# An attention block with inducing points and a gated feed-forward layer on one core: the inducing points on another queue, the weight casts on another engine, the next batch's loads placed later, and the written order redrawn

## The chip, the cores and the metric

The kernel runs on one core of a Trainium2 chip. The core has five engines that run side by side, each with its own list of instructions in order: TensorE (PE in the profile; PEld are its weight loads), VectorE (DVE), ScalarE (ACT), GpSimd (POOL) and SyncE (SP), which here only issues transfers. Transfers (DMA) run on 16 engines of their own. The metric is the device time of one execution in microseconds. The result below is judged against runs of the kernel before.

## The reference

Two stages follow each other. In the first, 32 inducing points attend to all 12416 tokens of a batch, giving a summary `h` of 32 rows, and each token then attends to these 32 rows. In the second, each token's result goes through a gated layer with 1536 hidden columns.

```python
def _attn_ref(x, inducing):            # x: 4 x 12416 x 128, inducing: 32 x 128
    def mab(q, kv):
        s = scale * (q @ kv.transpose(0, 2, 1))
        s = s - s.max(-1, keepdims=True)
        a = np.exp(s)
        a /= a.sum(-1, keepdims=True) + 1e-09
        return a @ kv
    h = mab(I, x)
    return mab(x, h)

def _moe_ref(x, w_gate, w_val, w_out): # 128 x 1536, 128 x 1536, 1536 x 128
    gate = 1.0 / (1.0 + np.exp(-(x @ w_gate)))
    val = x @ w_val
    return gate * val @ w_out
```

## The kernel before

**Tiles.** A batch has 97 blocks of 128 tokens. They are worked off as six quads of 16 blocks (the last has 17), and each quad as four units of 512 tokens; the odd block is a short 25th unit. So there are 4 batches of 24 full units and one short one.

**Stages.** For each quad, stage 1 (names `sa`, `hp`) scores the tokens against the inducing points, takes the exponential, and adds the weighted tokens to `hacc`. When all quads of a batch are done, `hT` is the batch's summary, and three folds (`fo`) multiply it with w_gate and w_val into `hw`, so that the second attention and the gated layer's first products become one product with 32 rows. Stage 2 (`sb`) scores the tokens against `hT`; the scores are transposed (`et`), summed by a tree on GpSimd (`tr`), divided (`rc`, `mu`), transposed back (`bt`), written to DRAM (`wr`) and read back four times (`re`), so that four row groups of TensorE can work at once. Then come the units: six products `G` for the gate and twelve `V` for the value, a tanh `T` on ScalarE for each G, a multiplication `D` on VectorE for each V (one in twelve goes through a copy `C` on ScalarE to GpSimd, `P`), twelve products `W` with w_out, a copy `E` and a store `st`.

**Prologue of batch 0.** Here the loads of x come as 32-bit numbers on SP (`lx`), are cast to 16 bits mostly on GpSimd (`cx`), transposed on TensorE (`xt`) and copied back (`xc`). The three weight matrices are loaded on SP too (`lwg`, `lwv`, `lwo`) and cast to 16 bits on GpSimd (`wg`, `wv`, `wo`), the last with a factor of 0.5. The inducing points (`lind`, 16 KB) are loaded on SP; `ind16`, `indT` and `indTc` turn them into the stationary matrix that every first score needs. The rows of quad 0 need no trip through DRAM: `rp` transposes them on TensorE and `rcp` copies them.

**Later batches.** A quad of x is loaded and cast in one transfer on GpSimd's queue (`ld`, into one of four buffers), and transposed by four transfers on SP (`xd`; five for the last quad). Stage 1 of a batch runs between the units of the batch before.

**Order.** Each operation is registered with an engine, a planned duration, its dependencies and a function that emits it. `ORDER` gives every engine's list by hand; `play` walks these lists with the planned durations, finds each operation's planned start, and the kernel emits all operations sorted by it. Each engine thus executes its list exactly as written, and an operation that waits holds up everything behind it on its engine. The waits on the chip themselves come from the data: who writes a tile, who reads it, and when a buffer is free. A dependency that is listed for `play` alone changes planned times, and no wait on the chip.

In the names, `ld1.2` is quad 2 of batch 1, `G0.4.0` the first gate product of unit 4 of batch 0. Every instruction that goes through the helper class `Eng` has line 626 in the profile.

Of the kernel before, what the change touches and what calls it, by code (L numbers as in the profile page):

```python
# [17 lines left out]
QS = 16  # L18
# [7 lines left out]
        xt0.8 xt0.0 indT xt1.8 sa0.0 xt1.0 ap0 xt2.8 sa0.1 xt2.0 hp0.0 ap1 xt3.0 sa0.2 hp0.1 xt3.8 ap2 xt4.0 hp0.2 sa0.3  # L26
        xt4.8 xt5.0 xt5.13 ap3 sa0.4 xt5.8 s1t0 ap4 s1t13 hp0.3 hp0.4 s1t8 hbase hsu0 hva0 hsu8 hva8 hsu13 hva13 s2t1
        s2t0 fo0.0 fo0.2 fo0.1 rp3 sb0.1 rp1 rp0 G0.0.0 V0.0.2 G0.0.1 V0.0.1 V0.0.8 G0.0.4 G0.0.5 V0.0.9 sa1.0 V0.0.0
        G0.0.2 G0.0.3 rp2 W0.0.2 V0.0.4 V0.0.5 G0.1.1 V0.0.7 G0.1.0 W0.0.8 W0.0.0 V0.1.0 G0.2.0 V0.0.3 V0.0.6 W0.0.4
        G0.1.5 G0.1.2 V0.0.11 V0.0.10 W0.0.9 V0.1.2 V0.1.5 G0.1.3 W0.0.11 sb0.2 W0.0.6 V0.1.3 V0.1.4 G0.2.3 V0.1.6  # L30
        W0.0.10 W0.0.7 G0.2.1 V0.1.10 W0.0.5 G0.1.4 V0.1.1 W0.0.1 V0.2.2 V0.1.7 G0.3.0 W0.0.3 V0.1.11 V0.2.7 V0.2.0
        G0.3.3 W0.1.1 W0.1.3 W0.1.4 G0.2.2 V0.1.8 W0.1.11 G0.2.5 V0.1.9 V0.2.5 W0.1.8 W0.1.9 G0.2.4 V0.2.4 hp1.0 G0.3.2
        V0.2.1 W0.1.7 W0.1.6 V0.3.0 V0.2.3 G0.3.4 W0.1.10 V0.2.9 W0.1.5 W0.1.0 V0.3.4 G0.3.1 V0.2.6 W0.1.2 V0.3.3 V0.3.2
        G0.3.5 V0.2.10 W0.2.4 W0.2.1 V0.2.8 V0.3.5 G0.4.0 W0.2.7 V0.4.0 G0.4.4 W0.2.8 W0.2.6 W0.2.0 G0.4.1 V0.2.11
        W0.2.2 V0.3.1 V0.3.6 G0.4.5 W0.2.10 W0.2.9 W0.2.3 G0.4.2 V0.3.8 W0.2.5 V0.4.2 V0.3.7 W0.2.11 sa1.1 V0.4.3 V0.4.4
        G0.4.3 W0.3.2 V0.4.1 W0.3.7 V0.3.9 G0.5.0 W0.3.5 V0.3.10 G0.5.1 V0.3.11 W0.3.3 W0.3.1 V0.4.6 G0.6.0 V0.4.9
        W0.3.0 W0.3.10 V0.4.5 G0.5.5 W0.3.4 W0.3.8 V0.4.7 G0.5.2 V0.4.8 W0.3.9 W0.3.11 W0.3.6 V0.4.10 V0.5.1 sb0.3
        G0.6.1 W0.4.4 W0.4.0 V0.5.5 G0.5.3 V0.5.0 V0.5.6 W0.4.6 W0.4.5 sa1.2 W0.4.7 V0.4.11 G0.6.3 V0.5.2 W0.4.8 W0.4.2
        G0.7.0 V0.5.3 V0.5.11 W0.4.1 V0.5.4 V0.5.7 G0.5.4 W0.4.10 W0.4.9 W0.4.3 V0.6.3 V0.6.2 G0.7.3 V0.5.10 W0.4.11
        V0.6.0 G0.6.2 V0.5.9 V0.5.8 V0.6.7 G0.6.4 W0.5.0 W0.5.1 W0.5.8 G0.6.5 V0.6.4 V0.6.5 W0.5.7 W0.5.5 G0.7.4 V0.6.1  # L40
        W0.5.6 hp1.1 G0.7.2 V0.6.6 W0.5.2 W0.5.10 G0.7.1 V0.7.0 V0.6.11 W0.5.4 W0.5.9 W0.5.11 W0.5.3 V0.7.4 V0.6.9
        G0.7.5 sa1.3 V0.7.2 W0.6.11 W0.6.3 V0.7.3 G0.8.0 V0.6.8 W0.6.7 V0.6.10 W0.6.2 V0.7.5 V0.8.0 G0.8.1 W0.6.6 W0.6.1
        V0.7.8 G0.8.4 W0.6.8 W0.6.4 V0.7.1 G0.8.5 V0.8.2 W0.6.10 W0.6.0 W0.6.5 W0.6.9 V0.8.1 G0.8.2 V0.7.7 G0.8.3 V0.7.6
        W0.7.1 W0.7.2 W0.7.8 V0.8.4 V0.8.3 W0.7.3 G0.9.0 V0.7.10 W0.7.4 G0.9.1 V0.7.9 V0.7.11 W0.7.10 W0.7.6 V0.8.5
        G0.10.0 V0.8.7 W0.7.0 G0.9.5 V0.8.9 W0.7.7 G0.9.2 V0.8.8 V0.8.6 W0.7.5 W0.7.11 W0.7.9 V0.9.0 G0.9.3 V0.9.1 sb0.4
        V0.8.10 W0.8.0 W0.8.3 V0.9.5 V0.9.2 G0.10.1 W0.8.2 hp1.2 sa1.4 V0.8.11 G0.10.3 V0.9.11 W0.8.5 V0.9.6 G0.11.0
        W0.8.4 W0.8.1 G0.10.2 V0.9.7 V0.9.4 W0.8.11 W0.8.7 W0.8.8 G0.9.4 V0.9.10 W0.8.6 V0.10.2 V0.9.3 W0.8.9 W0.8.10
        V0.9.8 G0.11.3 V0.10.3 G0.10.5 V0.10.0 W0.9.1 W0.9.4 V0.10.5 V0.10.4 W0.9.6 W0.9.5 W0.9.7 V0.9.9 G0.10.4 V0.10.7
        W0.9.0 V0.10.1 G0.11.4 W0.9.8 hp1.3 G0.11.1 V0.10.6 W0.9.11 W0.9.3 V0.11.0 V0.10.11 G0.11.2 W0.9.2 W0.9.10
        W0.9.9 G0.11.5 V0.10.9 V0.11.4 sa1.5 V0.11.2 W0.10.6 W0.10.2 V0.11.3 G0.12.0 V0.10.8 W0.10.5 W0.10.3 V0.10.10  # L50
        W0.10.1 V0.11.5 G0.12.1 V0.11.8 W0.10.0 W0.10.4 V0.12.0 G0.12.4 W0.10.9 W0.10.7 V0.11.1 V0.12.2 G0.12.5 W0.10.8
        W0.10.10 W0.10.11 V0.12.1 V0.11.6 G0.12.2 G0.12.3 V0.11.7 W0.11.1 W0.11.0 W0.11.2 V0.11.10 G0.13.0 V0.12.4
# [1105 lines left out]
```

## Time and profile before

| | |
|---|---|
| median of three runs | 737.59 us (733.43 to 741.64) |
| the profiled execution, its time | 733.21 us |
| the profiled execution, its span | 731.4 us |
| busy in it: TensorE, VectorE, ScalarE, GpSimd | 679.9, 677.7, 681.0, 342.6 us |
| mean granted TensorE clock | 0.984 |

The span is cut into 40 slices of 18.3 us on the profile's page, with the busy share of each engine in tenths. A line of the chain of waits gives start, duration and what was going on; a line of the timeline gives start, time from the first to the end of the last of the merged instructions, engine, operation and tiles (out<-in), and in brackets how long the engine had stood before, and what ended it. In a list of transfers the last number is the microseconds from issue to landing. SPq and POOLq are the issuing instructions of a queue.

### The profile page before, as it was taken

The page shows a single profiled execution, that of the slowest core. Times are in us where ns is not written, and L with a number is a line of the kernel's source. Part 1 is how long each engine was busy: PE and PEld are TensorE (multiplying, and loading weights), DVE is VectorE, ACT ScalarE, POOL GpSimd, SP SyncE. Part 2 cuts the span into 40 slices and gives each one's busy share as a digit, 9 for nine tenths or more (in the row PEclk, how much of TensorE's full clock was granted, in tenths as well). Part 3 has the DMA queues.
Part 4 walks back from the last instruction along what each step waited for, and adds up shares of the span by engine and source line. Part 5 has one row for each costly group of instructions (what it writes and reads, how often), then busy time and mean ns, then how long its engine had stood idle before and what let it go on. Part 6 is the DMA issues. An engine that isn't in the chain of part 4 may idle for free.

```text
span 731.4 us, 20034 instructions
## 1 busy us (share of the span) xinstructions
PE 679.9 (93%) x7928; PEld 381.4 (52%) x7928; DVE 677.7 (93%) x1156; ACT 681.0 (93%) x881; POOL 342.6 (47%) x452
## 2 busy tenths in 40 slices
PE   1749999999999999999999999999999999999997
PEld 0514555555555555555555555555545555555555
DVE  0448999999999999999999999999999999999997
ACT  1449999999999999999999999999999999999994
POOL 6335562562653552653644635526355345436332
PEclk9958999999999999999999999999999999999999
DMA  9594568665264754554545382331232221332111
GB/s 362 149 131 86 104 151 182 119 113 120 74 154 87 152 137 95 118 120 99 117 129 98 78 155 86 92 104 34 83 93 69 78 80 45 95 93 63 35 73 48
DMA packets 113327, 78.63 MB, mean 107 GB/s; under 512 B 80561, under 2 KB 97361, under 8 KB 112593
## 3 DMA queue, kind: packets, MB, share of 16 engines
q1 hardware_dynamic: 110640, 67.81, 37.0%
q0 software_dynamic: 2592, 9.54, 8.1%
q8 instruction: 62, 1.02, 0.6%
q14 instruction: 33, 0.26, 0.1%
HBM read 39.99 MB, written 28.57 MB: 94 GB/s over the span
## 4 chain that ended last, share of the span: by engine, by line
PE 50%; DVE 20%; ACT 15%; DMA 6%; issue 6%; POOL 2%; SPq 1%; ACTq 0%; POOLq 0%; DVEq 0%
PE acc L626 24%; DVE ua L626 19%; PE v L626 17%; ACT tga L626 12%; PE g L626 8%; DMA ind<-in_inducing_dram 2%; DMA xT<-x 2%; ACT os L626 2%; DMA out_dram<-os 1%; ACT vs L626 1%; SPq L626 1%; DMA xT<-in_x_dram 1%; POOL pt L626 1%; POOL ua L626 1%; ACT eT L626 0%
## 5 line engine op out<-in xcount | busy, mean ns | idle before, releaser
L626 DVE SCALAR_TENSOR_TENSOR ua<-tga,v 128x512 f16<-128x512 f16 x1056 | 648.5, 681 | 18.7 <-PE g L626 7.5
L626 ACT ACTIVATE tga<-g 128x1024 f16<-128x1024 f32 x576 | 562.4, 1078 | 5.1 <-PE v L626 1.8
L626 PE MATMUL acc<-wo,ua 128*128 128x128 f16 x4608 | 360.6, 221 | 2.0 <-DVE ua L626 0.3
L626 PEld LDWEIGHTS <-ua 128*128 128x128 f16 x4608 | 261.8, 98 | 172.6 <-issue 162.7
L626 PE MATMUL v<-a2r,hw 32*128 32x512 f16 (+1 forms) x1200 | 329.2, 376 | 12.5 <-DVE ua L626 10.0
L626 POOL TENSOR_TENSOR pt<-tga,vs 128x512 f32<-128x512 f16 x96 | 111.7, 1164 | 294.4 <-ACT vs L626 167.0
L626 PE MATMUL g<-a2r,hw 32*128 32x512 f16 (+1 forms) x1200 | 227.1, 380 | 4.1 <-ACT tga L626 2.0
L626 PEld LDWEIGHTS <-hw 32*128 32x128 f16 x2400 | 89.5, 91 | 116.4 <-issue 49.3
L626 POOL TENSOR_TENSOR ua<-pt,vs 128x512 f16<-128x512 f32 x96 | 121.7, 1268 | 7.5
L626 ACT COPY os<-acc 128x512 f32<-128x512 f32 (+1 forms) x100 | 62.3, 623 | 7.1 <-PE acc L626 6.7
L626 ACT COPY vs<-v 128x512 f32<-128x512 f32 x96 | 60.4, 630 | 0.2 <-PE v L626 0.2
L626 POOL TENSOR_TENSOR a2n<-e2t,rc 128x128 f16<-128x128 f16 x96 | 37.2, 484 | 18.3 <-DVE rc L626 17.5
L626 ACT ACTIVATE eT<-g 128x512 f16<-128x512 f32 (+1 forms) x26 | 15.5, 609 | 22.7 <-PE g L626 22.7
L626 POOL TENSOR_TENSOR tree<-e2t 128x256 f32<-128x256 f16 (+1 forms) x23 | 15.8, 687 | 24.2 <-DMA e2t<-e 24.2
L626 POOL TENSOR_TENSOR tree<-tree 128x64 f32<-128x64 f32 (+4 forms) x69 | 23.7, 344 | 5.4
L626 DVE CAST ind<-ind 32x128 f16<-32x128 f32 x1 | 0.2, 214 | 19.7 <-DMA ind<-in_inducing_dram 19.7
L626 ACT ACTIVATE e<-g 128x512 f16<-128x512 f32 (+1 forms) x23 | 16.2, 703 | 0.0
L626 PE MATMUL g<-xT,indT 128*32 128x512 f16 (+1 forms) x104 | 11.1, 393 | 5.3 <-DMA xT<-x 5.0
L626 POOL DMA_DIRECT2D x<-in_x_dram x18 | 10.6, 590 | 11.5 <-PE g L626 5.8
L626 PE MATMUL v<-ident,x 128*128 128x128 f16 x97 | 9.4, 258 | 6.9 <-POOL x L626 6.9
L626 ACT CAST hw<-g 128x1024 f16<-128x1024 f32 x11 | 11.7, 1076 | 0.8 <-PE g L626 0.7
L626 PEld LDWEIGHTS <-x 128*128 128x128 f16 x114 | 7.9, 113 | 8.6 <-POOL x L626 7.1
(77 smaller groups left out, 155.8 us busy)
## 6 DMA issues: line engine op xcount, KB each, us to landing
out_dram<-os SPq DMA_DIRECT2D x96, 256.0 KB, 2.3
a2r<-dr SPq DMA_DIRECT2D x92, 128.0 KB, 3.0
x<-in_x_dram POOLq DMA_DIRECT2D x15, 512.0 KB, 5.6
xT<-in_x_dram SPq DMA_DIRECT2D x3, 1024.0 KB, 9.0
dr<-a2p SPq DMA_DIRECT2D x19, 128.0 KB, 1.9
x<-in_x_dram POOLq DMA_DIRECT2D x3, 544.0 KB, 5.9
xT<-x SPq DMA_TRANSPOSE x75, 2.8
tga<-in_x_dram SPq DMA_DIRECT2D x1, 1024.0 KB, 5.0
```

The costliest lines, as they stand in the source:

```text
L626: ins = fn(*a, **k)
```

## The change

1. The inducing points are loaded by a transfer on ScalarE's queue, first in its list, instead of the tenth on SP's.
2. The weights are cast by ScalarE (two copies and one activation with scale 0.5) instead of GpSimd. In ScalarE's list `wg` stands behind `xsa0.4`, `wv` and `wo` behind the exponentials of stage 1's last quad and ahead of `xsb0.1`.
3. The loads of batch 1 get other planned conditions: quads 0 and 1 behind the cast of w_out, quads 2 to 5 behind the first tanh of units 0, 3, 6 and 9.
4. Planned durations and landings are changed, `play` keeps the loads of the prologue in the order of their registration, and all lists are redrawn. The starts of the lists, cut to what the text speaks of:

```diff
 "PE"
-xt0.8 xt0.0 indT xt1.8 sa0.0 xt1.0 ap0
+xt0.0 xt0.8 xt1.0 xt1.8 indT sa0.0 xt2.0
...
-ap3 sa0.4 xt5.8 s1t0 ap4 s1t13 hp0.3 hp0.4 s1t8 hbase hsu0 hva0 hsu8 hva8 hsu13 hva13 s2t1 s2t0 fo0.0 fo0.2 fo0.1 rp3 sb0.1 rp1 rp0
-G0.0.0 V0.0.2 G0.0.1 V0.0.1 V0.0.8 G0.0.4 G0.0.5 V0.0.9 sa1.0
+xt5.0 sa0.4 xt5.13 ap3 hp0.2 ap4 s1t8 s1t13 hp0.3 hp0.4 s1t0 hbase hsu0 hva0 hsu8 hva8 hsu13 hva13 sb0.1 fo0.1 s2t1 s2t0 fo0.2 fo0.0 rp0 rp1
+G0.0.2 V0.0.4 G0.0.0 V0.0.1 V0.0.0 G0.0.4 G0.1.2 G0.0.1 V0.0.8 V0.0.9 W0.0.4
...
+G0.1.4 V0.1.8 W0.1.7 V0.3.3 W0.1.4 W0.1.1 sa1.0
 "ACT"
-xc0.8 xsa0.0 xc1.8 xsa0.1
+lind xc0.8 xc1.8 xsa0.0 xsa0.1
...
-xs2t1 xs2t0 fc0.0 fc0.2 rcp3 xsb0.1 rcp1 T0.0.0 T0.0.1 T0.0.4 T0.0.5 xsa1.0
+xsa0.4 wg xs1t8 xs1t13 xs1t0 wv wo xsb0.1 xs2t1 xs2t0 fc0.2 fc0.0 rcp1 T0.0.2 T0.0.0
...
+C0.1.3 xsb0.2 T0.2.4 T0.2.0 rcp3 E0.0 T0.2.3 T0.3.0 T0.2.1 T0.3.1 T0.1.4 C0.3.3 xsa1.0
 "DVE"
-hr0 hc0 es1 er1 es0 en1 er0 en0 fc0.1 rcp0 D0.0.2
+hr0 hc0 fc0.1 es0 er0 es1 en0 er1 en1 rcp0 D0.0.4
 "POOL"
-cx5.0 cx5.8 ld1.0 ld1.1 wg ld1.2 wv wo ld1.3 tr0.1 mu0.1 P0.0.3 P0.1.3 tr0.2 P0.2.3 mu0.2 P0.3.3 P0.4.3 ld1.4
+cx5.8 cx5.0 ld1.0 ld1.1 tr0.1 mu0.1 ld1.2 P0.0.3 P0.1.3 ld1.3 tr0.2 P0.2.3 P0.3.3 mu0.2 P0.4.3 ld1.4
 "SP"
-lx4.0 lx5.8 lx5.0 lx5.13 lwg lind lwo lwv xd1.0.2 xd1.0.0 xd1.0.3 xd1.0.1 et0.1 xd1.1.0 xd1.1.2 xd1.2.3 at1.0
+lx4.0 lx5.0 lx5.8 lx5.13 lwg lwv lwo et0.1 xd1.0.3 xd1.0.1 bt0.1 xd1.0.2 xd1.0.0 xd1.1.0 wr0.1 et0.2 xd1.1.2 xd1.2.3 re0.1.2
```

The code around the lists:

```diff
-                if any(d.start is None for d in o.deps):
+                if any(d.start is None for d in o.deps) or (o.behind and o.behind.start is None):
...
-        return op("SP", 0.6, [], name, lambda o: SP.dma_start(dst, src), tail=max(2.0, landed[0] - landed[1]))
+        loads.append(op("SP", 0.6, [], name, lambda o: SP.dma_start(dst, src), tail=max(2.0, landed[0] - landed[1]), behind=loads[-1]))
+        return loads[-1]
...
+            if b == 0 and p == 0 and u % 3 == 0:
+                paced[2 + u // 3] = a
...
-    ld = load(ind32[:], inducing, 40000, "lind")
+    ld = op("ACT", 0.6, [], "lind", lambda o: ACT.dma_start(ind32[:], inducing), tail=3.0)
...
-        wl[nm] = op("POOL", 1.7, [ld], nm, lambda o, n=n, dst=dst: POOL.tensor_copy(out=dst, in_=WS[n]))
+        wl[nm] = act(F, [ld], nm, lambda o, n=n, dst=dst: ACT.copy(out=dst, in_=WS[n]))
...
-    wl["wo"] = op("POOL", 2.3, [ld], "wo", lambda o: POOL.tensor_scalar(
-        out=wo[:].rearrange("p j c -> p (j c)"), in0=WS[2], scalar1=0.5, scalar2=None, op0=ALU.mult))
+    wl["wo"] = act(F, [ld], "wo", lambda o: ACT.activation(
+        out=wo[:].rearrange("p j c -> p (j c)"), in_=WS[2], func=AF.Copy, scale=0.5))
...
-                    load_quad(b, i, [c for _, _, c in xload[0, NQ - 1][1]] if b == 1 else [])
+                    load_quad(b, i, ([wl["wo"]] if i < 2 else [paced[i]]) if b == 1 else [])
```

The other planned values that change are durations of the prologue's products on TensorE (from 0.08 to between 0.026 and 0.056 us for each block, and the like) and landings of transfers.

More of the change, by code (lines that the diff above doesn't have):

```diff
@@ L25 @@
     "PE": """
[L26 to L40, printed above, removed]
@@ L299 @@
-        C3.22.3 T3.22.5 T3.22.4 T3.23.4 T3.23.2 C3.23.3 E3.21 T3.24.1 T3.23.1 T3.23.5 T3.24.0 E3.22 E3.23 E3.24
+        lind xc0.8 xc1.8 xsa0.0 xsa0.1 xc2.8 xc3.8 xsa0.2 xc4.8 cx5.15 xsa0.3 xc5.8 xsa0.4 wg xs1t8 xs1t13 xs1t0 wv wo
+        xsb0.1 xs2t1 xs2t0 fc0.2 fc0.0 rcp1 T0.0.2 T0.0.0 T0.0.4 T0.1.2 T0.0.1 T0.0.3 C0.0.3 T0.0.5 T0.1.1 T0.1.0 T0.1.5
+        T0.1.3 C0.1.3 xsb0.2 T0.2.4 T0.2.0 rcp3 E0.0 T0.2.3 T0.3.0 T0.2.1 T0.3.1 T0.1.4 C0.3.3 xsa1.0 T0.2.2 C0.2.3
+        T0.2.5 E0.1 T0.3.3 T0.3.4 T0.3.5 T0.3.2 T0.4.0 T0.4.1 T0.4.4 T0.4.5 T0.4.2 E0.2 T0.4.3 T0.5.0 C0.4.3 xsa1.1
@@ L995 @@
     vcount = [0]
-    evac = []
+    evac, paced = [], {}
     def unit(b, u):
```

783 lines of the change are left out of this document (397 added, 386 removed).

## The prediction

> **What bounds the kernel now.** I read the slices of the page first, then busy time in chosen stretches, then the chain that ended last.
>
> ```profile
> span 731.4 us, 20034 instructions
> ...
> ACT  1449999999999999999999999999999999999994
> ```
> ```profile
> core 0: us, PE busy (x) PEld busy (x) DVE busy (x) ACT busy (x) POOL busy (x), PEclk, DMA share, GB/s
> 8.90:21.20 12.30, 0.03 (x1) 0.03 (x1) 0.30 (x2) 0.05 (x1) 5.44 (x6) 1.00 1.03 399
> ...
> 49.12:55.02 5.90, 0.87 (x7) 0.23 (x6) 0.74 (x2) 0.00 (x0) 0.17 (x1) 0.50 1.31 154
> 60.00:700.00 640.00, 622.76 (x7192) 346.51 (x7192) 631.15 (x1071) 636.45 (x818) 310.04 (x406) 1.00 0.44 102
> 700.00:731.40 31.40, 27.29 (x332) 17.37 (x330) 26.16 (x43) 21.19 (x27) 7.30 (x6) 0.97 0.12 45
> ```
>
> From 60 us to 700 us ScalarE is busy 636.45 of 640 us: it is the bound there, and a new order of the same work can win back 3.55 us at most. What is loose lies ahead of 60 us: in 8.90 to 21.20 TensorE, VectorE and ScalarE all stand, and in 49.12 to 55.02 ScalarE does nothing. The chain names both waits:
>
> ```profile
> 8.22 12.66 DMA ind<-in_inducing_dram
> ...
> 20.90 0.23 DVE ind L626
> ...
> 41.77 12.46 DMA xT<-x
> ...
> 54.27 0.67 PE g L626 x3
> ```
>
> First the 16 KB of inducing points; then a transposing transfer of the next batch, for whose scores (sa1.0) TensorE waits with batch 0 queued behind.
>
> **Part 1: the inducing points on ScalarE's queue.** Before, they are the tenth transfer on SP's queue.
>
> ```profile
> 0.74 1.28 ACT L626 ACT_TABLE_LOAD   x1 [0.74 <-PEq L1142]
> ...
> 2.94 2.04 SPq L626 DMA_DIRECT2D ua<-in_x_dram  x4
> ...
> 5.73 0.33 SPq L626 DMA_DIRECT2D tga<-in_moe_w_gate_dram  x1
> ...
> 8.22 0.34 SPq L626 DMA_DIRECT2D ind<-in_inducing_dram  x1
> ...
> 10.74 2.03 POOL L626 CAST x<-xT 128x1024 f16<-128x1024 f32 x2 [0.45 <-DMA xT<-in_x_dram]
> ...
> 13.18 4.91 SPq L626 DMA_DIRECT2D tga<-in_moe_w_val_dram  x1
> ```
> ```profile
> tga<-in_moe_w_gate_dram SPq DMA_DIRECT2D x1, 768.0 KB, 14.9
> ...
> tga<-in_moe_w_val_dram SPq DMA_DIRECT2D x1, 768.0 KB, 12.0
> ...
> ua<-in_x_dram SPq DMA_DIRECT2D x1, 256.0 KB, 14.2
> ```
>
> After, they are ScalarE's first instruction. It can go out at 0.74 us, or at 2.02 behind the table load. It lands at the latest after the 12.66 us that it took before, so by 14.7, and I take that it lands with the first load of x, by 5.8 (the load of w_gate goes out at 5.73, when that one is done), because nothing is queued ahead of it. TensorE's new list asks for it after four transposes of quads 0 and 1; quad 1 is cast when quad 2's cast begins, at about 10.5. So nothing waits for it, and no instruction of ScalarE is late: its first copy needs a transpose.
>
> [...] No row of before has a transfer on ScalarE's queue.
>
> With the points there, quads 0 to 3 are worked off as they land, one per 2.5 us, each cast in 2.03 us. The new end of the prologue is set by the last piece of x: the last of four issues in 2.94 to 4.98 starts near 4.5, plus 14.2 gives 18.7. From there I use rows of the old ending:
>
> ```profile
> 29.51 0.94 DVE L626 CAST x<-ua 128x512 f16<-128x512 f32 x3
> 29.62 0.41 ACT L626 CAST x<-ua 128x256 f16<-128x256 f32 x1
> ...
> 30.70 0.75 POOL L626 DMA_DIRECT2D x<-in_x_dram  x1 [0.99 <-PE g L626]
> ...
> 34.66 0.54 POOL L626 DMA_DIRECT2D x<-in_x_dram  x1 [3.21 <-PE acc L626]
> ...
> 36.89 0.29 DVE L626 TENSOR_TENSOR hT<-acc,rsb 128x128 f16<-128x128 f32 x1
> ...
> 37.73 0.66 ACT L626 ACTIVATE eb<-v 128x384 f16<-128x384 f32 x2 [2.41 <-PE v L626]
> ...
> 38.55 4.12 POOL L626 TENSOR_SCALAR wo<-hw 128x1536 f16<-128x1536 f32 x1
> ...
> 39.06 1.93 ACT L626 CAST hw<-g 128x1024 f16<-128x1024 f32 x2 [0.68 <-PE g L626]
> 39.13 3.09 DVE L626 TENSOR_TENSOR nb<-eb,rb 128x384 f16<-128x384 f16 x1
> ...
> 42.34 0.29 DVE L626 TENSOR_TENSOR nb<-eb,rb 128x128 f16<-128x128 f16 x1
> 42.55 1.22 DVE L626 CAST hw<-g 128x1024 f16<-128x1024 f32 x1
> ...
> 44.22 0.42 DVE L626 COPY a2r<-v 128x512 f16<-128x512 f16 x1 [0.46 <-PE v L626]
> ```
> ```profile
> 45.35 3.77 ACT L626 ACTIVATE tga<-g 128x1024 f16<-128x1024 f32 x4 [0.84 <-PE v L626]
> ```
>
> 18.7 plus VectorE's three casts (0.94) is 19.6. Before, hT was done (36.89 + 0.29 = 37.18) 6.73 us after the last cast (30.45); the same again gives 26.4.
>
> **Part 2: the weights on ScalarE.** One cast: the 1024-wide ones to hw take 0.97 each (1.93 / 2), the 256-wide cast 0.41, so 0.73 ns per element and 1.34 us for 1536; three cost about 4.0 us. All lie ahead of the first tanh, where ScalarE has gaps, so the stretch from 60 us on gets none of it. w_gate lands at 5.73 + 14.9 = 20.6, before ScalarE asks. That cast stands ahead of the last three exponentials of stage 1; it may push hT from 26.4 to 27.8 (upper bound), and nothing if it falls in a gap, which I take. The third weight is now w_out; the last weight landed at 13.18 + 12.0 = 25.2, and I use that. ScalarE's list has the w_out cast ahead of the next exponentials (xsb0.1, xs2t1, xs2t0), so these wait for 25.2 + 1.34 = 26.5 or later. What GpSimd gives up: two casts and the 4.12 us cast of w_out, which ran beside VectorE's nb of 3.09 us, where the piece a third as wide took 0.29; without it I count 3 x 0.29 = 0.87 for nb, bounded by 3.09.
>
> **Part 3: the next batch's loads.** The new conditions (behind the w_out cast, behind a paced tanh) enter only the planned times: emission uses the written list, the buffers' readers and data. So loads 1.0 and 1.1 keep their place right behind the last casts on GpSimd, and go out when hp0.2 and hp0.3 free their buffers (before: 30.70 and 34.66, the second 2.5 us ahead of hT). After, I put them at 23 and 24. They then share the DMA engines with w_out, of which up to 25.2 - 23 = 2.2 us are left; shared by halves these take twice as long: w_out lands at 25.2 at the best, 27.4 at the worst; I take 26.4, as the first load also needs time to start. The cast ends at 27.7, xsb0.1 costs about 0.5, with a gap the exponentials (eb) begin at 28.8 (bounds: 27.1 without either delay, 29.6 with both), and end 0.66 later, 29.5. VectorE then has two sums, two reciprocals and two products: 0.55 before for the wide sum (next fence), 0.6 together for the three small ones (an estimate by their widths), 0.29 + 0.87 for the products, 2.3 in all: 31.8. From the copy of a2r to the first tanh it was 45.35 - 44.22 = 1.13. **First tanh at 32.9** (bounds 31.2 and 33.7) instead of 45.35: 12.45 us earlier.
>
> ```profile
> 38.25 0.55 DVE L626 TENSOR_REDUCE sb<-eb 128x12 f32<-128x384 f16 x1 [1.06 <-ACT eb L626]
> ```
>
> The fold that VectorE copies (1.22) now stands ahead of those sums; it begins about when hT and two products of TensorE are done, near 28, and ends by 29.3, under eb.
>
> Load 1.2 really is later: behind mu0.1 instead of between weight casts; 1.3 to 1.5 stand behind products of units 1, 4 and 7.
>
> **Part 4: the new table.** TensorE's list has sa1.0 after 18 G's instead of 4. Four tanhs took 3.77 us, so 18 take 17.0, and ScalarE's list has six shorter pieces between (three copies, an exponential, a row copy, one output), 0.41 for 256 elements and 0.19 for 256 more, 0.6 each: the wait would come at 32.9 + 20.6 = 53.5. The transposes that it needs are placed behind et0.1 and around bt0.1 on SP:
>
> ```profile
> 36.14 7.17 SPq L626 DMA_TRANSPOSE xT<-x  x4
> ...
> 54.85 0.66 POOL L626 TENSOR_TENSOR tree<-e2t 128x256 f32<-128x256 f16 x1 [11.65 <-DMA e2t<-e]
> ...
> 60.22 1.55 POOL L626 TENSOR_TENSOR a2n<-e2t,rc 128x128 f16<-128x128 f16 x4 [3.18 <-DVE rc L626]
> ```
> ```profile
> x<-in_x_dram POOLq DMA_DIRECT2D x4, 512.0 KB, 9.0
> xT<-x SPq DMA_TRANSPOSE x8, 9.0
> e2t<-e SPq DMA_TRANSPOSE x1, 10.7
> ```
>
> The landings in the second fence are those of 30 to 60 us, with four loads in flight. Worst: et0.1 goes out at 28.3 and lands 10.7 later, at 39; tree, reciprocal and products take what they took from 54.85 to 61.77, 6.9, then bt0.1 and the last two transposes are issued (7.17 / 4 = 1.8 each, 5.4), and the last needs 9.0 to land: 60, which is 6.8 too late, and that wait would be as long as the old one. With two loads in flight rather than four I halve both landings: about 51, in time, by little. I take that nothing is left of the 5.90 us. Late next is then the replicated rows of unit 4 (re0.1), on the same chain. rcp3, a row copy of 0.6 us on ScalarE, moves behind the first tanh: +0.6. For the remaining order I take 0: it can win 3.55, and the list keeps its distances (35 to 40 G's between a quad's second score and its first use, in both tables, from batch 1 on).
>
> **Sum.** The profiled execution took 733.21 us, 1.8 above its span of 731.4. 733.21 - 12.45 - 5.90 + 0.6 = 715.5. The four known executions (733.21, 733.43, 737.59, 741.64) have their middle at 735.5, 2.3 above the profiled one, which the runs of after should share: **718 us** against the median of 737.59.
>
> **Rivals.**
> - A, the wait moves: SP's list is in order and stands at bt0.1 until GpSimd's products are done, and again at transposes of load 1.2. If that chain is as slow as in the rows with four loads, sa1.0 or the first G of unit 4 stops TensorE for up to 6.8 us, more than the 5.90 removed; at the worst the forecast plus 6.8: 725. For it: landings of 9.0 and 10.7. Against: fewer loads in flight.
> - B, the move to ScalarE's queue brings only the issue time: the points land 12.66 us after 2.02, at 14.7, and the 16.3 us of work that followed them before (20.90 to 37.18) put hT at 31.0, 4.6 later than counted: 723. [...] For it: the 12.66 us themselves. Against: those were spent behind megabytes issued earlier on the same queue.
> - C, slower than before: the new table makes ScalarE wait in the long stretch. It runs 96 full units, and decides at (737.6 - 718) / 96 = 0.20 us per unit; for slower by over 1%, 0.28. Before, ScalarE's idle time there was 3.55 us, 3.55 / 92 = 0.04 per unit of the some 92 in it. For it: every list is redrawn, and VectorE has only 8.85 us free in 640. Against: the same work and distances. At 0.3 per unit it gives 747; half of this, 732.
>
> **How the numbers follow.** Forecast 0.60, A 0.20, B 0.08, C 0.12 (0.07 within 1%, 0.05 slower). The runs of before lie 8.2 us apart, so about 1% (730.2 to 745.0) is what can be told from no change. Forecast, A and B are faster by more: 0.88. Low end: first tanh at 31.2 (-1.7), 3.5 won in the long stretch, a run like the profiled one: 710, and 709 for rounding of the parts. High end: A with a run as far up as the highest (8.4): 715.5 + 6.8 + 8.4 = 731, of which I leave off the last 2, where both mishaps must meet: 729. It leaves out C and a remnant of A.
>
> **What would show it.** The points' landing before 10 us and no stretch of 12 us without TensorE; w_out's cast on ScalarE near 27 and nb under 1 us; loads 1.0 and 1.1 on GpSimd near 23, not after the w_out cast; the first tanh at 31 to 34; no gap over 1 us on ScalarE from there to 60; and idle time of about 3.5 us per 640 from then on. Wrong it would be through a gap at sa1.0 or unit 4, or through idle time spread over all units.

## The result, and the profile after

| | before | after |
|---|---|---|
| median, us | 735.51 (733.25 to 741.64, 4 runs) | 714.11 (712.57 to 714.54, 4 runs) |
| the profiled execution, its time and span | 733.21, 731.4 | 714.31, 712.5 |
| its mean granted TensorE clock | 0.984 | 0.988 |

After takes 0.9692 of the time of before (95% interval 0.9627 to 0.9758): 3% less. The forecast was 718 us, the range 709 to 729. In the experiments below the medians go over all executions, the ranges leave out two at 838.33 us (experiment 2) and 814.6 us (experiment 7), and the ratios leave out every execution in a slow state, so that a median and its ratio need not match.

The page of after, its span, ScalarE's busy tenths in 40 slices of 17.8 us, and the granted clock of TensorE in the same slices:

```profile
span 712.5 us, 20005 instructions
...
ACT  3989999999999999999999999999999999999994
...
PEclk9959999999999999999999999999999999999999
```

The first three slices, 1 4 4 before, are 3 9 8. The 5 in the last row is taken up below. Busy times of after in chosen stretches (columns as in the prediction's first such table):

```profile
10.00:20.00 10.00, 9.20 (x118) 6.50 (x116) 4.91 (x10) 5.64 (x11) 7.32 (x9) 1.00 1.02 417
...
25.00:30.00 5.00, 3.31 (x62) 1.79 (x61) 3.05 (x8) 4.63 (x7) 0.00 (x0) 1.00 0.97 189
30.00:35.00 5.00, 2.92 (x47) 0.94 (x47) 2.93 (x6) 4.64 (x6) 1.89 (x5) 0.95 0.49 93
35.00:40.00 5.00, 5.00 (x50) 2.16 (x46) 3.62 (x7) 4.39 (x6) 1.41 (x4) 0.50 0.02 5
40.00:45.00 5.00, 5.00 (x37) 2.39 (x36) 3.63 (x7) 3.95 (x5) 3.04 (x4) 0.50 0.74 110
45.00:50.00 5.00, 4.65 (x47) 2.11 (x43) 3.16 (x6) 4.04 (x7) 2.99 (x4) 0.50 1.04 170
...
31.65:60.00 28.35, 26.00 (x232) 12.27 (x230) 21.05 (x34) 25.69 (x33) 13.84 (x23) 0.70 0.72 118
...
60.00:681.00 621.00, 604.53 (x7033) 338.21 (x7029) 614.66 (x1043) 618.42 (x794) 297.24 (x389) 1.00 0.44 102
```

TensorE now works 9.20 of the 10 us from 10 to 20 in which it stood before. From 60 us on ScalarE is idle for 621 - 618.42 = 2.6 us, as little as before. The timeline of after, with the lines that answer to the quoted ones of before:

```profile
0.74 0.42 ACTq L625 DMA_DIRECT2D ind<-in_inducing_dram  x1
...
10.75 0.39 SPq L625 DMA_DIRECT2D hw<-in_moe_w_out_dram  x1
...
18.87 1.60 DVE L625 CAST x<-ua 128x512 f16<-128x512 f32 x3
...
23.23 1.37 POOL L625 DMA_DIRECT2D x<-in_x_dram  x2 [2.91 <-PE v L625]
...
26.23 0.29 DVE L625 TENSOR_TENSOR hT<-acc,rsb 128x128 f16<-128x128 f32 x1
26.24 1.48 ACT L625 ACTIVATE wo<-hw 128x1536 f16<-128x1536 f32 x1 [0.23 <-DMA hw<-in_moe_w_out_dram]
...
28.10 0.65 ACT L625 ACTIVATE eb<-v 128x384 f16<-128x384 f32 x2
28.23 1.32 SPq L625 DMA_TRANSPOSE e2t<-e  x1
...
30.10 0.56 DVE L625 TENSOR_TENSOR nb<-eb,rb 128x384 f16<-128x384 f16 x1
...
31.65 1.95 ACT L625 ACTIVATE tga<-g 128x1024 f16<-128x1024 f32 x2
31.88 0.67 POOL L625 TENSOR_TENSOR tree<-e2t 128x256 f32<-128x256 f16 x1 [7.28 <-DMA e2t<-e]
```
```profile
55.07 0.64 ACT L625 ACTIVATE eT<-g 128x512 f16<-128x512 f32 x1
```

The first tanh starts at 31.65 instead of 45.35: 13.70 us won. The exponential of sa1.0 (55.07) has no bracket, so ScalarE did not wait for it. And the transfers up to 30 us, the last number being us from issue to landing:

```profile
hw<-in_moe_w_out_dram SPq DMA_DIRECT2D x1, 768.0 KB, 15.5
...
ind<-in_inducing_dram ACTq DMA_DIRECT2D x1, 16.0 KB, 3.5
```

Where the time went, in the two profiled executions: up to the first tanh 13.70 us; from there to the end 731.4 - 45.35 = 686.05 against 712.5 - 31.65 = 680.85, so 5.20 us, which is the 5.90 us wait less the 0.6 us of rcp3, to 0.1 us. Two other things cancel within it. From the first tanh to 60 us ScalarE of after is idle for 28.35 - 25.69 = 2.66 us, nearly all of it while the granted clock is 0.50, where before it was idle for 0.59 us beside the wait; from 60 us to the end it is idle for 11.82 us, before for 13.76. Together 18.9 us. The medians lie 21.4 us apart; the 2.5 us between these two figures come from which execution was profiled, 2.3 us below the median in before and 0.2 us above it in after. TensorE's clock may make such differences (experiment 6), but for these runs it is not shown: the clocks of before's other executions are not known.

### The profile page after: what moved, and what is told of

The parts are those of the page before. It is cut to its first block, busy times and chain, and to the rows that moved or that the text cites. A ratio compares the mean times of both kernels' runs of the same rounds, so it can differ in the third digit from the quotient of the medians.

```text
span 712.5 us, 20005 instructions
## 1 busy us (share of the span) xinstructions
PE 679.3 (95%) x7928; PEld 382.2 (54%) x7928; DVE 677.4 (95%) x1156; ACT 685.2 (96%) x884; POOL 336.5 (47%) x449
## 4 chain that ended last, share of the span: by engine, by line
PE 56%; DVE 27%; ACT 11%; issue 5%; DMA 1%; POOL 0%; ACTq 0%; SPq 0%; DVEq 0%
PE acc L625 27%; DVE ua L625 25%; PE v L625 20%; PE g L625 9%; ACT tga L625 8%; ACT os L625 2%; DMA xT<-in_x_dram 1%; ACT vs L625 1%; DVE ut L625 1%; ACT eT L625 0%; ACT hw L625 0%; ACT tgt L625 0%; ACT e L625 0%; DVE xT L625 0%; DVE hw L625 0%
## 5 line engine op out<-in xcount | busy, mean ns | idle before, releaser
L625 DVE SCALAR_TENSOR_TENSOR ua<-tga,v 128x512 f16<-128x512 f16 x1056 | 648.7, 680 | 13.7 <-PE v L625 3.7
L625 ACT ACTIVATE tga<-g 128x1024 f16<-128x1024 f32 x576 | 562.0, 1078 | 3.5 <-PE v L625 1.0
L625 PE MATMUL acc<-wo,ua 128*128 128x128 f16 x4608 | 362.4, 221 | 1.3
L625 PEld LDWEIGHTS <-ua 128*128 128x128 f16 x4608 | 262.6, 98 | 170.1 <-issue 160.9
L625 PE MATMUL v<-a2r,hw 32*128 32x512 f16 (+1 forms) x1200 | 327.6, 377 | 12.4 <-DVE ua L625 9.6
L625 POOL TENSOR_TENSOR pt<-tga,vs 128x512 f32<-128x512 f16 x96 | 111.7, 1164 | 296.8 <-ACT vs L625 208.6
L625 PE MATMUL g<-a2r,hw 32*128 32x512 f16 (+1 forms) x1200 | 227.0, 381 | 4.7 <-ACT tga L625 3.1
L625 PEld LDWEIGHTS <-hw 32*128 32x128 f16 x2400 | 89.7, 91 | 120.3 <-issue 55.7
L625 POOL TENSOR_TENSOR ua<-pt,vs 128x512 f16<-128x512 f32 x96 | 121.8, 1268 | 7.5
L625 ACT COPY os<-acc 128x512 f32<-128x512 f32 (+1 forms) x100 | 62.3, 623 | 6.8 <-PE acc L625 6.8
L625 ACT COPY vs<-v 128x512 f32<-128x512 f32 x96 | 60.9, 634 | 1.6 <-PE v L625 1.2
L625 POOL TENSOR_TENSOR a2n<-e2t,rc 128x128 f16<-128x128 f16 x96 | 37.2, 485 | 25.2 <-DVE rc L625 22.2
L625 POOL TENSOR_TENSOR tree<-tree 128x64 f32<-128x64 f32 (+4 forms) x69 | 23.8, 344 | 5.4
L625 POOL TENSOR_TENSOR tree<-e2t 128x256 f32<-128x256 f16 (+1 forms) x23 | 15.9, 690 | 20.2 <-DMA e2t<-e 20.2
L625 ACT ACTIVATE eT<-g 128x512 f16<-128x512 f32 (+1 forms) x26 | 15.7, 613 | 1.6 <-PE g L625 1.5
L625 PE MATMUL v<-ident,x 128*128 128x128 f16 x97 | 9.8, 270 | 7.4 <-POOL x L625 7.4
L625 ACT ACTIVATE e<-g 128x512 f16<-128x512 f32 (+1 forms) x23 | 15.8, 687 | 0.0
L625 DVE COPY xT<-v 128x1024 f16<-128x1024 f16 (+1 forms) x7 | 4.5, 651 | 11.7 <-PE v L625 11.6
L625 ACT COPY xT<-v 128x1024 f16<-128x1024 f16 (+1 forms) x6 | 5.8, 959 | 9.4 <-PE v L625 9.4
L625 PEld LDWEIGHTS <-x 128*128 128x128 f16 x114 | 8.4, 119 | 9.0 <-POOL x L625 8.5
L625 POOL DMA_DIRECT2D x<-in_x_dram x18 | 10.7, 596 | 3.0 <-PE v L625 2.9
L625 ACT CAST hw<-g 128x1024 f16<-128x1024 f32 x11 | 11.6, 1059 | 0.1
```

Source lines behind the costliest of these rows:

```text
L625: ins = fn(*a, **k)
```

## The experiments

Each ratio is to runs of before on the same chip. L625 to L639 in the lines is the helper class in each kernel's own numbering. "Half clock" stands for stretches in which the granted clock is 0.50; a mean clock c over a span s is worth about 2 x (1 - c) x s us of it (0.988 over 712.5 us gives 17.1 us for after, whose profile has 0.50 from 34.5 to 51.6).

**1. The points alone (`e1_points`).** Before, and only:

```diff
-    ld = load(ind32[:], inducing, 40000, "lind")
+    ld = op("ACT", 0.6, [], "lind", lambda o: ACT.dma_start(ind32[:], inducing), tail=3.0)
 "ACT"
+lind xc0.8 xsa0.0 ...
 "SP"
-lx5.13 lwg lind lwo lwv
+lx5.13 lwg lwo lwv
```

> The kernel before, with the inducing points alone moved: first in ScalarE's list, on ScalarE's queue. Theory (three waits in a row, each worth its own time): the first tanh comes near 34.5 us instead of 45.35, since the weight casts on GpSimd still run beside nb; the wait at sa1.0 stays, 6 to 9 us, because the next batch's loads and transposes move forward with the prologue. About 723 us. Rival (the points save only issue time): they land near 14.7 us and the time is 726 to 728. Rival (the next batch's loads now collide with the weights, so that the gain is eaten): first tanh near 39, 728 or more.

724.39 us (722.12 to 726.69), ratio 0.9802 (0.9727 to 0.9877). The first tanh came at 36.16, 9.2 us earlier. The total was as expected, but not the way to it. ScalarE's timeline:

```profile
36.16 3.77 ACT L638 ACTIVATE tga<-g 128x1024 f16<-128x1024 f32 x4 [0.84 <-PE v L638]
39.83 0.60 ACT L638 ACTIVATE eT<-g 128x512 f16<-128x512 f32 x1
```

The exponential of sa1.0 follows the first four tanhs without a bracket: the wait is gone, though the score stands where it stood. What was lost instead lay at the old cast of w_val on GpSimd (TensorE stood 3.7 us for it ahead of a fold) and in a longer half clock, from 40 to about 63 us, in which ScalarE had gaps (busy 7.52 of 10 us from 50 to 60). So the points' queue is the larger part of the gain: some 16 us of medians on this chip (740.4 for before; 14.7 by the ratio), of 21.

**2. The weight casts alone (`e2_weights`).** Before, with the three casts as ScalarE's, at `xsa0.4 wg xs1t0` and `xs1t13 wv wo xs2t1` in its list, and taken out of GpSimd's.

> The kernel before, with the three weight casts alone moved from GpSimd to ScalarE. Theory: nb falls from 3.09 us to under 1, the first tanh comes about 2 us earlier (43.2), but sa1.0 still waits for transposes that land near 54, so the time is the same as before within 1 us. Rival (the gain of 2 us goes through to the end): 2 us less than before.

733.96 us (728.05 to 738.61), ratio 0.9966 (0.9919 to 1.0013): no difference that can be told. The first tanh came 0.64 us earlier (44.71) and ScalarE's wait at sa1.0 shrank from 5.9 to 3.3 us, but the half clock lasted until about 71 us. The product nb took 0.54 us, as expected, but ScalarE's casts now stand ahead of the exponentials eb, which began at 39.30 instead of 37.73: most of what nb won was lost again there.

**3. The score later (`e3_late_score`).** Before, with sa1.0 and its exponential 14 gate products later, as in after:

```diff
 "PE"
-G0.0.5 V0.0.9 sa1.0 V0.0.0
+G0.0.5 V0.0.9 V0.0.0
...
+W0.1.4 G0.2.2 sa1.0 V0.1.8
 "ACT"
-T0.0.5 xsa1.0 T0.0.2
+T0.0.5 T0.0.2
...
+T0.3.3 T0.2.2 xsa1.0 T0.2.5
```

(hp1.0, ha1.0 and at1.0 are put later in the same manner.)

> The kernel before, with sa1.0 alone moved from after 4 gate products to after 18 (its exponential, its transpose at1.0 and hp1.0 behind it). Theory: the gap of 5.9 us at 49 us goes; the rows of unit 4, which landed near 75.6, come up to 2 us late next, so the time falls by 4 to 6 us. Rival (the wait only moves): a gap of 4 us or more at the first product of unit 4, and under 2 us gained.

738.28 us (732.03 to 742.94), ratio 0.9972 (0.9924 to 1.0019): the 4 to 6 us did not come. Its timeline shows the wait elsewhere:

```profile
55.93 0.66 POOL L638 TENSOR_TENSOR tree<-e2t 128x256 f32<-128x256 f16 x1 [12.47 <-DMA e2t<-e]
...
58.16 0.25 DVE L638 RECIPROCAL rc<-sm 128x16 f32<-128x16 f32 x1 [4.50 <-POOL sm L638]
...
61.03 1.02 ACT L638 ACTIVATE tga<-g 128x1024 f16<-128x1024 f32 x1 [3.65 <-PE g L638]
```

Read upwards: ScalarE waited 3.65 us for TensorE, because VectorE stood 4.50 us at the reciprocal of quad 1, because GpSimd's tree waited for the transposed scores, which landed 11 us after their issue, four loads being in flight. This is the prediction's rival A, at another operation than it named. The rest went into half clock, up to 78 us (ScalarE is busy 14.58 of the 20 us from 60 to 80 at a mean clock of 0.55, in before 19.68 at 1.00).

**4. The three together, in the old lists (`e4_three`).** The edits of 1, 2 and 3 in one kernel. GpSimd's list then has four loads of batch 1 side by side.

> The kernel before, with these three edits together, but without the redrawn table and with the next batch's four loads where they were on GpSimd (now directly behind each other, as no weight cast is between them). Theory: the three edits carry the gain and the redrawn table nothing: 714 to 717 us, first tanh near 32.5. Rival (the later place of loads 1.2 and 1.3 counts): with four loads in flight the transposes land late, a gap of 3 us or more at sa1.0 or unit 4, 719 or more.

722.34 us (720.49 to 724.77), ratio 0.9766 (0.9707 to 0.9825). The first tanh came at 37.10, not at 32.5, and the list of ScalarE's waits between 30 and 120 us begins with the reason:

```profile
ACT wv L638 <- DMA tga<-in_moe_w_val_dram: 3.7, 1, 3.7
```

w_val landed 18.1 us after its issue (12.0 before), with four loads beside it. Which of the loads does it is not isolated: experiment 8 issues 1.2 and 1.3 later, and its last weight lands later still. What experiments 1, 4 and 8 share is a first load at 19.11 to 20.00 us and a last weight at 28.7 to 31.3; in after the load goes out at 23.23 and the weight lands at 26.2. So 37.10 - 31.65 = 5.45 us at the first tanh, and 6 to 8 us of the time (720.49 against 714.31 in the profiled executions, 722.34 against 714.11 by medians on different chips), are not in the three named edits but in the lists around them.

**5. After once more (`n1_after_again`), 6. after with a busier TensorE (`n2_warm`).** The second adds 41 products of 128 columns ahead of named operations near the first tanh; nobody reads what they write.

```diff
+WARM = {'sb0.1': 8, 'fo0.2': 4, 'rp0': 6, 'rp1': 3, 'V0.0.0': 2, 'G0.0.4': 6, 'G0.1.2': 6, 'G0.0.1': 6}
...
+        for _ in range(WARM.get(o.name, 0)):
+            PE.matmul(ACC[:, 384:512], lhsT=ident[:], rhs=ones16[:], start=True, stop=True, skip_group_check=True)
```

> The changed kernel once more, on the same chip as the others of this call and of the four parts before. Every theory: 712 to 715 us, mean granted TensorE clock 0.988 or above.

> The changed kernel with 41 more products into an unused part of ACC, in the gaps of TensorE between 25.8 and 34.5 us (before sb0.1, fo0.2, rp0, rp1, V0.0.0, G0.0.4, G0.1.2, G0.0.1). Theory (idle time of TensorE around the first products halves its granted clock from 34.5 to about 51 us, and ScalarE idles some 3 us there): the clock stays at 1.00, mean 0.998 or above, 711 to 712 us. Rival (the half clock is set by something else, or costs nothing because ScalarE is the bound): clock and time as in the changed kernel, 713 to 715.

After: 714.47 us (712.09 to 719.2; mean clocks 0.985 to 0.995; the run at 719.2 had a wait of 3.9 us for a store in addition). With the added products: 711.46 (711.2 to 712.65; 0.995 to 0.998), ratio 0.9671 (0.9554 to 0.9789). Busy times of the second:

```profile
25.00:30.00 5.00, 4.14 (x50) 2.47 (x47) 1.99 (x4) 3.35 (x6) 0.00 (x0) 0.66 1.00 199
30.00:35.00 5.00, 4.65 (x69) 2.47 (x69) 2.93 (x9) 4.65 (x6) 1.89 (x5) 1.00 0.42 76
35.00:40.00 5.00, 4.71 (x58) 2.47 (x56) 4.74 (x10) 5.00 (x7) 1.34 (x4) 1.00 0.01 2
40.00:45.00 5.00, 4.87 (x51) 2.67 (x50) 4.51 (x8) 5.00 (x7) 4.21 (x5) 1.00 0.73 109
```

The clock is back at 1.00 by 30 us, and from 35 to 45 ScalarE is busy 10.00 of 10 us, where after's profile at the top had 4.39 + 3.95 = 8.34. By the medians the half clock costs after 3.0 us, although the added products put the first tanh at 32.66, 1 us later; the ranges still touch (712.65 and 712.09). This is the fastest version of the study.

**7. The loads really held (`n3_real_hold`).** In after, the condition "behind the cast of w_out" is only planned; here GpSimd reads a corner of the cast weights first.

```diff
+            if b == 1 and i == 0:
+                POOL.tensor_copy(out=HOLD[:], in_=wo[0:1, 0, 0:2])
             POOL.dma_start(buf.t[:, 0:ns, :], xv[b][:, i * QS : i * QS + ns, :])
```

> The changed kernel, with a real wait on the w_out cast ahead of the loads 1.0 and 1.1 on GpSimd (a copy of two elements of wo). Theory (the plan's condition holds nothing back, the loads go out near 23 us and share the DMA engines with w_out): now they go out near 28; w_out lands up to 1 us earlier, and the first tanh comes at most 0.3 us earlier, since ScalarE is busy with the w_val cast until 26.0; the transposes for sa1.0 still land in time: 713 to 715 us. Rival (the loads behind the w_out cast arrive too late): a gap of 2 us or more on ScalarE near 53 us, 716 or more.

712.69 us (711.79 to 712.99), ratio 0.9681 (0.9518 to 0.9844). From its timeline:

```profile
25.99 1.48 ACT L626 ACTIVATE wo<-hw 128x1536 f16<-128x1536 f32 x1
...
28.10 1.25 POOL L626 DMA_DIRECT2D x<-in_x_dram  x2 [0.39 <-PE v L626]
...
31.63 5.62 ACT L626 ACTIVATE tga<-g 128x1024 f16<-128x1024 f32 x6
```

The loads go out at 28.10 instead of 23.23, so after does not hold them. That w_out shares the DMA engines with them costs it 0.4 us (landed after 15.1 us here, 15.5 in after), and the first tanh nothing (31.63 and 31.65). The median lies 1.8 us below that of experiment 5, but the ranges overlap, and the runs have clocks of 0.992 to 0.995 where those had 0.985 to 0.995; a gain of the hold itself is not shown.

**8. Only two of the new lists (`n4_two_lists`).** Experiment 4, with GpSimd's and SP's lists of after.

> The kernel before with the three edits of the points, the weights and sa1.0, and with the lists of GpSimd and SyncE taken whole from the changed kernel; TensorE, VectorE and ScalarE keep the old lists but for the three edits. Theory (with four loads in flight behind the casts w_val and w_out landed late and the first tanh came at 37.1; placing loads 1.2 and 1.3 later cures that): first tanh near 32, 714 to 717 us. Rival (the redrawn lists of the three compute engines carry part of the gain): 719 or more.

754.4 us (748.11 to 756.26), ratio 1.0237 (1.0076 to 1.0397): slower than before. Its timeline:

```profile
20.00 0.72 POOL L638 DMA_DIRECT2D x<-in_x_dram  x1 [0.83 <-PE g L638]
...
31.34 1.48 ACT L638 ACTIVATE wo<-hw 128x1536 f16<-128x1536 f32 x1 [4.40 <-DMA hw<-in_moe_w_out_dram]
...
38.34 3.77 ACT L638 ACTIVATE tga<-g 128x1024 f16<-128x1024 f32 x4 [0.84 <-PE v L638]
...
40.07 0.66 POOL L638 TENSOR_TENSOR tree<-e2t 128x256 f32<-128x256 f16 x1 [15.58 <-DMA e2t<-e]
```

TensorE's old list frees the first buffer at 20.00 rather than 23.23; the load goes out 3 us earlier, w_out lands after 20.4 us, and ScalarE stands 4.40 us at its cast. The first tanh comes at 38.34, later than in experiment 4. The larger loss lies behind it: from there to the end it takes 746.3 - 38.34 = 707.96 us, 27 more than after. In the long stretch ScalarE's idle time comes up to 6.4 us per 100:

```profile
200.00:300.00 100.00, 92.10 (x1072) 51.24 (x1070) 92.06 (x156) 93.61 (x121) 44.46 (x59) 0.98 0.53 112
```

That is rival C, brought about here by mixing lists of different tables; through which operations was not followed. How what experiment 4 left is shared between the new lists stays open: these two, taken over alone, do not fit the others.

**9. After with the points back on SP's queue (`m1_points_back`).**

```diff
 "ACT"
-lind xc0.8 xc1.8
+xc0.8 xc1.8
 "SP"
-lx5.13 lwg lwv lwo
+lx5.13 lwg lind lwv lwo
```

> The changed kernel with the inducing points alone put back on SyncE's queue, tenth in its list behind w_gate; all other lists stay. Theory (the 12 us wait of TensorE is worth what it lasts): the points land near 21 us, hT comes near 35 instead of 26.5 and the first tanh near 40.5 instead of 31.6, so 722 to 725 us. Rival (in the new table the weights and the loads would bound the prologue anyway): first tanh before 36, under 719.

723.89 us (723.41 to 729.2), ratio 0.9818 (0.9771 to 0.9866); the first tanh, and the exponential of sa1.0:

```profile
40.39 5.71 ACT L639 ACTIVATE tga<-g 128x1024 f16<-128x1024 f32 x6
...
61.85 0.71 ACT L639 ACTIVATE eT<-g 128x512 f16<-128x512 f32 x1
```

In the chain of waits the points take 12.29 us (12.66 before). The exponential of sa1.0 has no bracket: in the new table the wait is gone even with the points back behind w_gate. Inside the new table their queue is worth 9.8 us of medians (723.89 against 714.11) and 8.74 us at the first tanh: less than the 16 of experiment 1. A part of those, the wait at sa1.0 among it, is thus won by the rest of the change as well.

**10. Before with a busier TensorE (`m2_before_warm`).** 97 such products in the kernel before, 50 of them ahead of sa1.0.

```diff
+WARM = {'s2t1': 8, 'fo0.1': 8, 'rp3': 14, 'G0.0.0': 6, 'G0.0.4': 8, 'G0.0.5': 3, 'sa1.0': 50}
```

> The kernel before with 97 more products into an unused part of ACC, in the gaps of TensorE between 36 and 54 us (50 of them ahead of sa1.0). Theory (the half clock of 20 to 50 us per execution costs about 0.27 us for each of them, and its varying length is what makes the kernel's runs differ): mean granted clock 0.995 or above, 727 to 731 us, runs within 3 us of each other. Rival (the runs differ by other things, such as transfers): the clock rises, but the runs still spread over 8 us or more, with a median of 733 or more.

742.98 us (733.08 to 747.28), ratio 0.9995 (0.9948 to 1.0042): wrong in time and in spread. TensorE's timeline in the profiled run, and two rows of busy times:

```profile
47.39 2.96 PE L628 MATMUL acc<-ones,ident 128*128 128x128 f16 x50
50.28 0.39 PE L628 MATMUL g<-xT,indT 128*32 128x512 f16 x1
60.43 0.61 PE L628 MATMUL g<-xT,indT 128*32 128x512 f16 x3 [9.76 <-DMA xT<-x]
```
```profile
50.00:60.00 10.00, 0.67 (x8) 0.27 (x6) 0.00 (x0) 0.00 (x0) 0.00 (x0) 0.66 1.24 66
60.00:70.00 10.00, 9.14 (x70) 3.63 (x69) 5.63 (x10) 8.03 (x11) 5.42 (x11) 0.50 0.58 81
```

The 50 products take 2.96 us and the wait 9.76: the clock falls within the wait, and stays at 0.50 beyond 90 us. Time and clock go together all the same: two runs at 0.991 and 0.992 took 733.1 us, seven at 0.979 or less 742.4 to 747.3. That does not say which is the cause, as a longer wait would lengthen both.

**11. Experiment 7 with the products of 6 (`m3_hold_warm`).**

> The changed kernel with both the real wait ahead of loads 1.0 and 1.1 and the 41 filling products: the two edits that were fastest so far. Theory: the hold moves w_out's landing by less than half a microsecond and the clock is already kept, so 710.5 to 712.5 us, as with the filling products alone. Rival (the hold has a gain of its own): under 710.

715.84 us (711.35 to 718.97), ratio 0.9688 (0.9637 to 0.9739): the two gains do not add up. Its profiled run:

```profile
39.85 0.66 POOL L628 TENSOR_TENSOR tree<-e2t 128x256 f32<-128x256 f16 x1 [9.99 <-DMA e2t<-e]
...
42.08 0.25 DVE L628 RECIPROCAL rc<-sm 128x16 f32<-128x16 f32 x1 [3.64 <-POOL sm L628]
...
42.93 0.58 PE L628 MATMUL v<-a2r,hw 32*128 32x512 f16 x1 [3.38 <-DVE ua L628]
```

The held loads run beside the transposed scores of quad 1, as in experiment 7. There the scores' transfer was issued at 27.98, just ahead of the loads at 28.10, and landed after 6.3 us; here the added products put it at 28.78, behind the loads at 28.61, and it lands after 11.0 us. (That this order makes the difference is read from the two traces, not tested.) VectorE stands at the reciprocal, TensorE behind it, and the clock is halved again from 42 to 56 us. The same chain as in experiment 3. So the early loads of after are worth something after all: they are out of the way of this transpose (3.6 us to land in after).

**12. Experiment 10 with 40 more products behind sa1.0 (`p1_refill`).**

```diff
-... 'sa1.0': 50}
+... 'sa1.0': 50, 'V0.0.0': 40}
```

> The kernel before with the fillers of m2_before_warm and 40 more of the same 128-wide products directly behind the score sa1.0, that is directly behind the long wait for the transposes after which the clock of m2_before_warm was halved (0.50 from 53.5 us to beyond 90 us in its profile, mean clock 0.971 to 0.974 in six of ten runs). Question: does full-size work on TensorE end the half clock, or does its length not depend on what TensorE does? At half clock 40 such products take about 4.7 us (50 took 2.96 us at full clock), during which ScalarE gets no new gate products. Theory F (a few us of products that use all 128 rows bring the clock back, while the products with 32 rows that make up the units do not): the granted clock is 1.00 some 4 us behind the long wait in the profile, the mean clock is 0.983 or more in nearly all runs, and the median is 737 to 740 us, since about 35 us of half clock saved are worth some 9 us against 4.7 us spent. Theory N (the length of the half clock does not depend on it): mean clocks spread as before, 0.965 to 0.99, and the median is 745 to 748 us, 4 to 5 us above the 742.98 us of m2_before_warm.

740.07 us (733.58 to 747.9), ratio 1.0027 (0.9982 to 1.0072). Six of the ten runs had a mean clock of 0.983 or more, three of them 0.997 or 0.998, which no run of before or of experiment 10 had; the other four had 0.973 to 0.982. That leans to theory F, but it isn't "nearly all", and the profiled run decides nothing: its wait at sa1.0 was short and the clock did not fall.

```profile
53.98 0.40 PE L628 MATMUL g<-xT,indT 128*32 128x512 f16 x3 [3.26 <-DMA xT<-x]
54.31 2.41 PE L628 MATMUL acc<-ones,ident 128*128 128x128 f16 x40
```

What ends a half clock stays open.

## Why the prediction was right, step by step

- **The points' queue.** Forecast: landed by 5.8, an estimate of the author's that no row of before shows, as none of its transfers is on ScalarE's queue. Measured: 0.74 + 3.5 = 4.2. The same 16 KB took 12.66 us in before, behind the loads on SP's queue. Rival B (landing 12.66 us after issue, at 14.7) is out; experiment 9, where they land near 20.5, bounds what it would have cost at 9.8 us.
- **hT** at 26.4; measured 26.52. The three casts of x ahead of it took 1.60 us instead of 0.94, beside a cast of GpSimd, and ended at 20.47 instead of 19.6; the old ending's 6.73 us became 26.52 - 20.47 = 6.05. The two errors nearly cancel.
- **The casts.** 1.34 us each; measured 1.46 to 1.48. w_out landed at 10.75 + 15.5 = 26.2 (forecast 26.4), and its cast began at 26.24. Two errors nearly cancel here too: with no load beside it, it would have landed at 10.78 + 15.1 = 25.9 (experiment 7), not at 25.2, and the loads cost it 0.4 us, not 1.2. nb at 0.56 and 0.28 us (forecast 0.87 and 0.29) where it took 3.09 beside GpSimd's cast.
- **The loads are not held.** Forecast 23 and 24; measured 23.23, both within 1.37 us. Experiment 7 holds them and wins nothing at the first tanh.
- **The first tanh** at 32.9; measured 31.65. Of the 1.25 us, 0.7 are the exponentials (28.10 instead of 28.8: w_out's cast ended at 27.72, as forecast, but the gap that I had added behind it did not come), and the rest is mostly VectorE's chain, 28.79 to 30.66 = 1.9 us instead of 2.3. This is the one term of the sum up to the profiled time whose errors did not cancel.
- **The wait at sa1.0.** It is gone without a remnant, as forecast, and the tree began at 31.88 where the bad case had the transposed scores land at 39. The forecast gave two reasons: the new table asks for the score later, and with fewer loads in flight the transfers land sooner. The later score alone wins nothing (experiment 3). The points alone remove the wait with the score in its old place (experiment 1), and the new table removes it with the points back behind w_gate (experiment 9), so either would have done. It goes with the landings: the transposing transfers took a median of 3.5 us in experiment 1 (20 to 52 us), 4.5 in experiment 9 (30 to 62) and 4.3 in after (20 to 52), but 9.0 in before and 7.9 in experiment 3 (30 to 62). Experiment 2, with 4.0 us and 3.3 us of the wait left, shows that the landings are not all of it.
- **The rest of the table** at 0: from the first tanh on the sum is met within 0.1 us. That closeness is luck: 2.07 us more idle time of ScalarE up to 60 us, at half clock, stand against 1.94 us less from there to the end, and the forecast had neither. Rival C did not appear in after, only in experiment 8.
- **The offset of 2.3 us** for other runs was wrong. The sum of 715.5 was 1.2 above the profiled run's 714.31, and the runs of after lie around that one (712.57 to 714.54), not above it. With the offset and the rounding these are the 3.9 us between 718 and 714.11. What the offset stood for was the spread of before's runs (8.4 us in the table above); the four of after there spread over 2.0 us, the five of experiment 5 over 7.1, the one at 719.2 making most of it.

**What the forecast left out: TensorE's clock.** The prediction's own rows showed it: 0.50 in 49.12 to 55.02. It was read as a side of the wait, not as a cost. Over 51 runs of before in the experiments' four series (one of 1039.21 us left out) the half clock lasts between 17 and 59 us, and a straight line through them gives 0.31 us per us of it (correlation 0.93). This is a fit, and it has a rival: a longer wait at sa1.0 would lengthen both the half clock and the time. ScalarE stood there 5.9 us in the profile of before, 13.1 in that of experiment 10 (745.83 us) and 6.4 in that of experiment 12 (734.55 us). A price can be read directly: in experiment 10 ScalarE is busy 8.03 + 7.51 + 7.21 of the 30 us from 60 to 90, at half clock throughout, so it loses 0.24 us per us. Experiment 6 is the test, for after: taking the half clock away wins 3 us by the medians. After has less of it in its runs (clocks 0.985 to 0.995) than before (0.960 to 0.988), which fits that the medians differ by more than the two profiled executions.

## What to carry to other kernels

A small transfer that everything waits for belongs on a queue with nothing ahead of it; look for it in the chain of waits, by a landing time out of proportion to its size (here 16 KB, 12.66 us behind the loads on SP's queue and 3.5 on ScalarE's). Before a waiting operation is moved back in an in-order list, follow what feeds it and its neighbours (here transfer, tree, reciprocal, VectorE's list) to the next engine that will stand: moving it alone may win nothing (experiment 3, ratio 0.9972). Read the granted clock in the stretch after each stall as a cost of its own: the stall may be paid for twice (in experiment 10 a wait of 9.76 us, and behind it 0.24 us of ScalarE's time per us of half clock).

## What the runs showed of the hardware that was not expected

**A half clock that outlasts the wait.** In experiments 10 and 11 the clock falls 2.4 and 2.6 us after TensorE's last product (it stood from 50.67 and from 39.55; the clock falls near 53.1 and 42.1), while the stand of 3.26 us in experiment 12 does not bring it down (1.00 in every stretch from 40 to 90 us). In after it falls near 34.5, behind 10 us in which TensorE was busy 3.31 + 2.92 us, with no stand above 0.8 us in the last 9 of them, and comes back near 51.6, 17 us later, though TensorE is busy 10.00 of 10 us from 35 to 45. In experiment 6 it was back after 3.4 us (25.8 to 29.2), of which TensorE was busy 3.1 with products that use all 128 rows, the added ones among them; in experiment 10 it was down for all of the 30 us of work from 60 to 90. What brings the clock down and what brings it back is thus not shown. Whether the units' products with 32 rows bring it back later than those with 128 was asked in experiment 12 and not settled.

**VectorE beside GpSimd.** VectorE's cast of three pieces took 1.60 us in after, beside casts of GpSimd that ran from 17.07 to 20.32 us, against 0.94 before, where GpSimd's casts ended 0.20 us into it. Its product nb took 3.09 us before, beside GpSimd's cast of w_out (38.55 to 42.67), against 0.56 in after and 0.54 in experiment 2, where ScalarE casts the weights. Why VectorE takes longer beside these casts is not shown.

**The price of a neighbour on the DMA engines.** w_out landed after 15.1 us with no load of batch 1 beside it (experiment 7), 15.5 with two loads from 23.23 us on (after), and 20.4 with the first load at 20.00 us (experiment 8). In experiment 8 the DMA engines were as busy beside the loads as without them, but moved half as much: a share of 1.07 and 412 GB/s from 16 to 18 us, 1.05 and 199 GB/s from 26 to 28.
